# Decode attention with grouped queries: the tokens of one value half are handed out ahead of GpSimd's wait for an output copy, and VectorE counts eight times behind its last sum

## The chip, the cores and the metric

The kernel runs on one core of one Trainium2 chip. The metric is the device time of one execution in microseconds (us), as a median of several executions. One more execution was profiled; all times inside the kernel come from it and count from the start of its span.

## The reference

One token is decoded: 32 query heads of 128 numbers, in 8 groups of 4 heads, each group with its own 65536 keys and values (bf16).

```python
B, Hq, Hkv, Sq, Sk, D = 1, 32, 8, 1, 65536, 128
k = jnp.repeat(k, Hq // Hkv, axis=1)
v = jnp.repeat(v, Hq // Hkv, axis=1)
scores = jnp.einsum("bhqd,bhkd->bhqk", q, k) * D ** -0.5
p = softmax(scores, axis=-1)
return jnp.einsum("bhqk,bhkd->bhqd", p, v)
```

Each key and each value is read once: 268 MB in all.

## The kernel before

**Tiles and their order.** The keys and the values of a group are read in two halves each, here called K(g,0), K(g,1), V(g,0), V(g,1). A half is 256 rows of 128 numbers on each of the 128 partitions, 8.4 MB. They go through a ring of three buffers, `buf`, in the order of the list `tiles` (L153 to L156): K(0,0), K(0,1), K(1,0), K(1,1), V(0,0), and then for each group from 2 on K(g,0), K(g,1), V(g-2,1), V(g-1,0). At the end come V(6,1), V(7,0) and V(7,1). SyncE issues all of these loads, on one queue. Before it issues a load it waits until the half that lies three places earlier has been used up (L163 to L169); for values this is the count `vit`, to which TensorE adds one for every 32 rows that it has consumed (L491).

**The stages of a group.** VectorE turns the keys in place (`turn`, L311), TensorE makes the scores in four PSUM banks (L462), VectorE takes maxima (L371), TensorE and VectorE find each head's maximum (L506, L384), and ScalarE makes the exponentials `E` and their sum (L242). VectorE transposes them into the weights `Ew`, in two halves (L316). TensorE then multiplies weights by values, 4 rows a matmul and 8 matmuls for each pass of the loop `values` (L481 to L494), into `psum_o`; VectorE picks the right blocks of `psum_o` (L324) and sums them (L332); TensorE picks the group's heads (L433), VectorE takes the reciprocal of the sum (L338), and ScalarE scales and writes the group's output (L249), which adds one to `outs`.

**TensorE's order.** TensorE runs these stages as blocks with branches. In turn g it makes the scores of group g, then (from g = 2) uses V(g-2,1), then runs the block `summed` (closing matmul L423, L506, clearing matmul L420, L433), and then uses V(g-1,0). The block `turn` (L516) comes next and takes one count of `wqs`. After V(6,0) there are no more scores: TensorE goes through `turn` and `late` straight to V(6,1), and after V(7,0) likewise to V(7,1). The first 192 rows of V(7,1) run in the loop, its next 40 rows in the block `tail` (L535), and its last 24 rows go one by one (L544).

**Tokens.** Before each pass of `values` TensorE takes one token from `sV` (L482), which stands for 32 rows that have landed. For most halves SyncE adds the eight tokens, in its own stream, when the landing is there (L168). For the last ones, V(6,0), V(6,1) and V(7,0), whose loads are split into 2, 3 and 4 pieces (`BY`), and for the first 4 of the 7 pieces of V(7,1) (`PIECES`, `MOVED`), GpSimd adds them piece by piece as each lands (L216 to L218). All tokens look alike, so those of V(6,0) may not be handed out while TensorE could still take them for V(5,1).

**GpSimd's stream.** GpSimd lays out the queries of group g for the scores once `outs` has reached g (L203 to L213) and adds one to `wqs` each time. Behind the eighth group it waits until `outs` has reached 8, that is until ScalarE has written the output of group 6, adds 2 to `wqs` (L214), and only then begins the list of tokens at L216.

**The end.** VectorE's last block (`last`, L388 to L404) has no loop: it counts on `dl` behind each picking step and waits for it ahead of the sum (L394, L395 and L401, L402). After the last sum TensorE picks group 7's heads, ScalarE scales them (L260) and issues the last store (L264), and counts on `fin` (L265); SyncE counts on `fin` once TensorE is done (L188). GpSimd waits for two counts on `fin` (L557), clears all semaphores (L558) and waits for the stores (L559).

Of the kernel before, what the change touches and what calls it, by code (L numbers as in the profile page):

```python
# [13 lines left out]
G = 8  # L14
# [3 lines left out]
NT = 256  # L18
# [3 lines left out]
BY = {  # L22
    (G - 2, 0): (128, 128), (G - 2, 1): (128, 64, 64), (G - 1, 0): (64, 64, 64, 64),
}
N = 2
STEP = 32
PIECES = (64, 64, 32, 32, 40, 16, 8)
MOVED = 4
# [3 lines left out]
def kernel(  # L32
# [18 lines left out]
    _, Hkv, Sk, _ = k.shape  # L51
# [5 lines left out]
    pe, dve, act, pool, sp = nc.tensor, nc.vector, nc.scalar, nc.gpsimd, nc.sync  # L57
# [38 lines left out]
    def sem(name):  # L96
        sems.append(nc.alloc_semaphore(name))
        return sems[-1]
# [3 lines left out]
    sL = [sem(f"sL{x}") for x in range(sum(map(len, BY.values())))]  # L102
    sP = [sem(f"sP{x}") for x in range(len(PIECES))]
# [5 lines left out]
    vit = sem("vit")  # L109
    scd = sem("scd")  # L110
    vdone = sem("vdone")
    wqs = sem("wqs")
# [7 lines left out]
    outs = sem("outs")  # L120
    rls = sem("rls")
    end = sem("end")
    dl = sem("dl")
# [3 lines left out]
    fin = sem("fin")  # L127
# [75 lines left out]
    for g in range(G):  # L203
# [7 lines left out]
            in1=quad[:, :].unsqueeze(1).unsqueeze(3).broadcast_to([P, 4, 4, H]),  # L211
            op=ALU.mult,
        ).then_inc(wqs, 1)  # L213
    pool.wait_ge(outs, G).then_inc(wqs, 2)  # L214

    for land, n in list(zip(sL, sum(BY.values(), ()))) + list(zip(sP, PIECES))[:MOVED]:  # L216

        pool.wait_ge(land, 32 if land is sP[0] else 16).then_inc(sV, n // STEP)  # L218

    def take(engine, semaphore, n=1):  # L220

        engine.wait_ge(semaphore, n).then_inc(semaphore, -n)  # L222
# [16 lines left out]
    for g in range(G + 1):  # L239
# [8 lines left out]
        at = max(g - 1, 0) * D  # L248
# [3 lines left out]
        if g == 0:  # L252

            for b in range(3):
                n = sum(kind == "k" and at % 3 == b and 0 < h < G - 1 for at, (kind, h, _) in enumerate(tiles))
# [57 lines left out]
    def weights(s):  # L313

        at = slice(1024 * s, 1024 * (s + 1))
        return dve.transpose(out=Ew[:, at], in_=E[:, at])  # L316

    def next_over():

        return dve.tensor_copy(out=rl, in_=rl_next)  # L320

    def picked():

        return dve.tensor_tensor(  # L324
            out=o_m[:, :].rearrange("p (y d) -> p y d", y=4),
            in0=psum_o[:, :].rearrange("p (y d) -> p y d", y=4),
            in1=pick[:, :].unsqueeze(2).broadcast_to([P, 4, D]),
            op=ALU.mult,
        )

    def summed():
        return dve.tensor_reduce(  # L332
            out=o_r[:, 0:D], in_=o_m[:, :].rearrange("p (y d) -> p d y", y=4), axis=AX.X, op=ALU.add
        )

    def over():

        dve.reciprocal(out=rl_next, in_=psum_f[0:H, D:D + 1]).then_inc(rls, 1)  # L338
# [49 lines left out]
    with block("last"):  # L388
        dve.wait_ge(exd, 1)
        dve.wait_ge(vit, NT // STEP * (2 * G - 3))  # L390
        weights(0)
        dve.wait_ge(vdone, 1)
        next_over().then_inc(mxs, 1)
        picked().then_inc(dl, 1)  # L394
        dve.wait_ge(dl, 1)  # L395
        summed().then_inc(mxs, 1)
        weights(1).then_inc(sP[0], 16)
        dve.wait_ge(pes, 2)
        over()
        dve.wait_ge(vdone, 2)  # L400
        picked().then_inc(dl, 1)  # L401
        dve.wait_ge(dl, 2)  # L402
        summed().then_inc(mxs, 1)
        dve.br("done")  # L404


# [49 lines left out]
    with block("scores"):  # L456
# [3 lines left out]
        for y in range(4 * N):  # L460
            m, n = y % 4, y // 4
# [64 lines left out]
    with block("tail"):  # L526
        at = sum(PIECES[:MOVED])
# [26 lines left out]

    pool.wait_ge(fin, 2).then_inc(fin, -2)  # L557
    nc.clear_and_free_semaphores(cleared)  # L558
    pool.wait_ge(sS, 32).then_inc(sS, -32)  # L559

# [29 lines left out]
```

## Time and profile before

| | us |
|---|---|
| median of 3 runs | 632.24 (631.0 to 632.6) |
| the profiled execution | 632.93 |
| its span, first to last instruction | 630.7 |
| TensorE busy (matmul) | 503.5 |
| VectorE busy | 337.9 |
| ScalarE busy | 21.1 |
| GpSimd busy | 5.9 |
| mean granted TensorE clock | 0.935 of full speed |

How to read it: the span is the time from the first to the last instruction in the trace, and the execution's own time is 2.2 us longer. "Busy" is the union of an engine's instructions; register, branch and semaphore instructions aren't in it, so a GpSimd that only hands out tokens counts as idle. PE is TensorE's matmul side and PEld its weight loads, DVE is VectorE, ACT ScalarE, POOL GpSimd, SP SyncE. A q behind an engine's name is its sequencer. L222 is the line of the helper `take`, so "PEq L222" means that TensorE's sequencer stood at such a wait. In a timeline row the square brackets hold the engine's idle time just before the row and what ended it.

### The profile page before, as it was taken

The page shows a single profiled execution, that of the slowest core. Times are in us where ns is not written, and L with a number is a line of the kernel's source. Part 1 is how long each engine was busy: PE and PEld are TensorE (multiplying, and loading weights), DVE is VectorE, ACT ScalarE, POOL GpSimd, SP SyncE. Part 2 cuts the span into 40 slices and gives each one's busy share as a digit, 9 for nine tenths or more (in the row PEclk, how much of TensorE's full clock was granted, in tenths as well). Part 3 has the DMA queues.
Part 4 walks back from the last instruction along what each step waited for, and adds up shares of the span by engine and source line. Part 5 has one row for each costly group of instructions (what it writes and reads, how often), then busy time and mean ns, then how long its engine had stood idle before and what let it go on. Part 6 is the DMA issues. An engine that isn't in the chain of part 4 may idle for free. (4 is left out here: it accounts for less than half of the span.)

```text
span 630.7 us, 8029 instructions
## 1 busy us (share of the span) xinstructions
PE 503.5 (80%) x2189; PEld 204.6 (32%) x2189; DVE 337.9 (54%) x118; ACT 21.1 (3%) x28; POOL 5.9 (1%) x16
## 2 busy tenths in 40 slices
PE   0685398898994979939799398994889987879998
PEld 0232043343331333314333133331333333323333
DVE  3984994789214882158721686217852688210100
ACT  1000100100010000100001000010000100010000
POOL 2000000000000000000000000000000000000000
PEclk9999599798998899988999798997999999898999
DMA  8999999999999999999999999999999999999995
GB/s 368 432 463 403 461 399 466 399 466 399 466 420 445 453 411 461 403 466 399 466 399 466 399 466 399 466 399 466 399 466 399 432 432 466 399 432 431 422 427 217
DMA packets 7000, 268.46 MB, mean 426 GB/s; under 512 B 856, under 2 KB 856, under 8 KB 1112
## 3 DMA queue, kind: packets, MB, share of 16 engines
q1 hardware_dynamic: 6912, 268.44, 98.8%
q10 hardware_dynamic: 88, 0.02, 0.0%
HBM read 268.44 MB, written 0.01 MB: 426 GB/s over the span
## 5 line engine op out<-in xcount | busy, mean ns | idle before, releaser
L311 DVE STREAM_TRANSPOSE buf<-buf 128x8192 f32<-128x8192 f32 x32 | 277.2, 8694 | 84.8 <-DVEq L222 84.8
L462 PE MATMUL sc<-buf,zeros 128*128 x1024 | 244.0, 396 | 0.0
L486 PE MATMUL psum_o<-buf,Ew 128*16 x1008 | 228.1, 385 | 13.6 <-PEq L222 9.7
L462 PEld LDWEIGHTS sc<-buf,zeros 128*128 x1024 | 101.6, 99 | 134.6 <-issue 38.7
L486 PEld LDWEIGHTS psum_o<-buf,Ew 128*16 x1008 | 90.2, 89 | 148.6 <-issue 55.1
L420 PE MATMUL sc<-zeros 128*128 128x512 bf16 x32 | 13.6, 426 | 87.2 <-PEq L222 87.0
L324 DVE TENSOR_TENSOR o_m<-psum_o,pick 128x512 f32<-128x512 f32 x10 | 7.0, 696 | 99.0 <-DVEq L222 72.1
L320 DVE COPY o_r<-o_r 4x1 f32<-4x1 f32 x9 | 1.3, 142 | 76.7 <-DVEq L222 64.1
L420 PEld LDWEIGHTS sc<-zeros 128*128 128x128 bf16 x32 | 3.1, 98 | 96.4 <-issue 95.4
L242 ACT ACTIVATE zeros<-sc,nmb 128x2048 bf16<-128x2048 f32 x8 | 15.7, 1967 | 536.6 <-DVE nmb L384 536.6
L316 DVE STREAM_TRANSPOSE Ew<-zeros 128x1024 bf16<-128x1024 bf16 x18 | 22.3, 1240 | 19.6 <-PE psum_o L486 19.5
L371 DVE TENSOR_REDUCE mx<-sc 128x1 f32<-128x2048 f32 x8 | 18.0, 2252 | 0.0
L506 PE MATMUL misc<-each,same 128*128 128x512 f32 x18 | 10.8, 685 | 8.3 <-PEq L222 8.3
L443 PE MATMUL misc<-qt,rep 32*128 32x128 bf16 x1 | 0.3, 281 | 10.6 <-DVE qt L301 10.6
L420 PE MATMUL psum_o<-zeros 128*128 128x512 bf16 x10 | 4.5, 446 | 5.3 <-PEq L222 5.3
L332 DVE TENSOR_REDUCE o_r<-o_m 128x128 f32<-128x512 f32 x10 | 6.9, 692 | 1.2
L208 POOL TENSOR_TENSOR zeros<-qx,quad 128x64 bf16<-128x64 bf16 x8 | 2.4, 294 | 487.6 <-ACT o_out L249 481.4
L506 PEld LDWEIGHTS misc<-each,same 128*128 128x128 f32 x18 | 2.9, 203 | 8.6 <-issue 8.5
L423 PE MATMUL sc<-zeros 128*128 128x1 bf16 x32 | 5.2, 163 | 0.0
L420 PEld LDWEIGHTS psum_o<-zeros 128*128 128x128 bf16 x10 | 1.0, 98 | 12.8 <-issue 12.6
L287 DVE CAST rep<-ident 32x128 bf16<-32x128 f32 x1 | 2.9, 2877 | 2.7 <-POOL ident L193 2.7
L423 PEld LDWEIGHTS sc<-zeros 128*128 128x128 bf16 x32 | 3.0, 95 | 3.9
(32 smaller groups left out, 37.3 us busy)
## 6 DMA issues: line engine op xcount, KB each, us to landing
buf<-in_k_dram SPq DMA_DIRECT2D x8, 4096.0 KB, 28.4
buf<-in_v_dram SPq DMA_DIRECT2D x8, 2048.0 KB, 34.4
buf<-in_v_dram SPq DMA_DIRECT2D x3, 4096.0 KB, 31.5
buf<-in_v_dram SPq DMA_DIRECT2D x2, 1024.0 KB, 32.7
buf<-in_v_dram SPq DMA_DIRECT2D x1, 1280.0 KB, 36.4
buf<-in_v_dram SPq DMA_DIRECT2D x1, 512.0 KB, 37.2
buf<-in_v_dram SPq DMA_DIRECT2D x1, 256.0 KB, 36.9
buf<-in_k_dram SPq DMA_DIRECT2D x12, 34.6
```

Source lines behind the costliest of these rows:

```text
L242: act.activation(out=E[:, :], in_=sc[:, :], func=ACT.Exp, bias=nmb[:, 0:1], scale=SCALE, accum_out=o_r[:, D:D + 1],).then_inc(exd, 1)
L287: dve.tensor_copy(out=rep[:, :].rearrange("p (a x) -> p a x", a=4), in_=ident[0:32, 0:32].unsqueeze(1).broadcast_to([32, 4, 32]),)
L311: dve.transpose(out=kv, in_=kv).then_inc(kt, 1)
L316: return dve.transpose(out=Ew[:, at], in_=E[:, at])
L324: return dve.tensor_tensor(out=o_m[:, :].rearrange("p (y d) -> p y d", y=4), in0=psum_o[:, :].rearrange("p (y d) -> p y d", y=4), in1=pick ...
L332: return dve.tensor_reduce(out=o_r[:, 0:D], in_=o_m[:, :].rearrange("p (y d) -> p d y", y=4), axis=AX.X, op=ALU.add)
L371: after(dve.tensor_reduce(out=mx[:, :], in_=sc[:, :], axis=AX.X, op=ALU.max))
L420: return pe.matmul(out=bank, lhsT=zer[:, 0:P], rhs=zer[:, :], start=True, stop=False)
L423: return pe.matmul(out=bank[:, 0:1], lhsT=zer[:, 0:P], rhs=zer[:, 0:1], start=False, stop=True)
L462: pe.matmul(out=bank, lhsT=moved(wq[:, m * SLIDE + 4 * n:][:, 0:P], slide), rhs=moved(T[:, n, m // 2, m % 2], keys), start=False, stop=False,)
L486: last = pe.matmul(out=psum_o[0:16, :], lhsT=moved(Ew[:, column(4 * j + 3):][:, 0:16], weight), rhs=moved(buf[:, 4 * j * D:][:, 0:4 * D], ...
L506: pe.matmul(out=misc[:, :], lhsT=same[:, :], rhs=each[:, :].unsqueeze(1).broadcast_to([P, 16, 32]), start=True, stop=True,).then_inc(pes, 1)
```

## The change

GpSimd's wait for `outs` and the 2 counts on `wqs` move from ahead of the list of tokens to behind its second entry, so behind both pieces of V(6,0). In their old place GpSimd now waits until `vit` has reached 8 * (2 * 8 - 4) = 96, that is until TensorE has used up every half as far as V(5,1). VectorE issues eight instructions more behind its last sum, each a bare count: seven on `dl` and one on `fin`. GpSimd's wait at the end asks for three counts on `fin` in place of two.

```diff
@@ GpSimd, behind the loop over the groups
-    pool.wait_ge(outs, G).then_inc(wqs, 2)
-
-    for land, n in list(zip(sL, sum(BY.values(), ()))) + list(zip(sP, PIECES))[:MOVED]:
+
+    pool.wait_ge(vit, NT // STEP * (2 * G - 4))
+    for at, (land, n) in enumerate(list(zip(sL, sum(BY.values(), ()))) + list(zip(sP, PIECES))[:MOVED]):
 
         pool.wait_ge(land, 32 if land is sP[0] else 16).then_inc(sV, n // STEP)
+        if at == 1:
+            pool.wait_ge(outs, G).then_inc(wqs, 2)
@@ VectorE, block "last"
         dve.wait_ge(dl, 2)
         summed().then_inc(mxs, 1)
+
+        for _ in range(7):
+            dve.nop().then_inc(dl, 1)
+        dve.nop().then_inc(fin, 1)
         dve.br("done")
@@ GpSimd, at the end
-    pool.wait_ge(fin, 2).then_inc(fin, -2)
+    pool.wait_ge(fin, 3).then_inc(fin, -3)
```

## The prediction

> **What bounds the kernel now.** I read the page first, for the transfers:
>
> ```profile
> DMA packets 7000, 268.46 MB, mean 426 GB/s; under 512 B 856, under 2 KB 856, under 8 KB 1112
> buf<-in_v_dram SPq DMA_DIRECT2D x1, 1280.0 KB, 36.4
> buf<-in_v_dram SPq DMA_DIRECT2D x1, 512.0 KB, 37.2
> buf<-in_v_dram SPq DMA_DIRECT2D x1, 256.0 KB, 36.9
> ```
>
> The first line says that 268 MB of keys and values fill nearly the whole span (630.7 us) at 426 GB/s. The other three are the last three pieces of V(7,1), the second half of group 7's values (40, 16 and 8 rows). The trace has SyncE issuing them at 585.60, 586.09 and 587.01, so they land at 622.0, 623.3 and 623.9. The span ends 6.8 us after the last landing, so the end isn't the transfers' alone. Hence the second view, TensorE's timeline near the end (start, length, line, what, count, idle before):
>
> ```profile
> 545.95 15.33 PE L486 MATMUL psum_o<-buf,Ew 128*16 x64 [3.05 <-PEq L222]
> 561.21 0.18 PE L423 MATMUL psum_o<-zeros 128*128 128x1 bf16 x1
> 561.25 1.10 PE L506 MATMUL misc<-each,same 128*128 128x512 f32 x2
> 563.22 0.38 PE L420 MATMUL psum_o<-zeros 128*128 128x512 bf16 x1 [0.87 <-PEq L222]
> 563.52 0.38 PE L433 MATMUL psum_f<-o_r,sel 128*4 128x129 f32 x2
> 567.09 30.50 PE L486 MATMUL psum_o<-buf,Ew 128*16 x128 [3.19 <-POOLq L218]
> 597.52 0.18 PE L423 MATMUL psum_o<-zeros 128*128 128x1 bf16 x1
> 600.18 14.19 PE L486 MATMUL psum_o<-buf,Ew 128*16 x64
> 615.39 10.72 PE L486 MATMUL psum_o<-buf,Ew 128*16 x48 [1.01 <-PEq L222]
> 626.27 0.82 PE L535 MATMUL psum_o<-buf,Ew 128*16 128x512 bf16 x10 [0.17 <-issue]
> ```
>
> From 567.09 on TensorE works without a long gap through V(6,0) and V(6,1) (128 matmuls), V(7,0) (64), 192 rows of V(7,1) (48) and the 40 rows of L535. It reaches those 40 rows at 626.27, 4.3 us after they landed. So in the last 60 us TensorE is late and the transfers are ahead. The one avoidable wait in that run is the 3.19 us before 567.09, and the view names what ended it: GpSimd's token at L218.
>
> Third, the stretches around it (busy of each engine, granted TensorE clock, DMA share, GB/s):
>
> ```profile
> 564.04:567.09 3.05, 0.00 (x0) 0.01 (x1) 0.31 (x3) 2.30 (x3) 0.00 (x0) 0.79 1.20 516
> 567.09:572.60 5.51, 5.51 (x14) 1.83 (x15) 0.00 (x0) 0.00 (x0) 0.00 (x0) 0.50 0.88 381
> 572.60:597.50 24.90, 24.90 (x116) 10.27 (x114) 1.25 (x1) 0.00 (x0) 0.00 (x0) 1.00 1.01 431
> ```
>
> After the wait the first 5.5 us run at half clock, 0.43 us a matmul instead of 0.216. So the wait costs more than its own length.
>
> **The change, part by part.**
>
> *The tokens of V(6,0).* Before, GpSimd stands at L214 until ScalarE has scaled group 6's output (that copy ends at 566.63, the wait at 566.67) and hands out tokens at 566.76 and 566.86. Now it waits for the value count 96, which TensorE reaches with the last matmul of V(5,1) at 561.27, then for the landings. In the trace's landing records V(6,0)'s two halves land at 555.3 and 565.0. So the first four tokens are there by about 561.5, before TensorE asks at about 563.8, and the other four at 565.1. When TensorE needs none of this wait, the same step is seen one group earlier:
>
> ```profile
> 489.68 0.17 PE L423 MATMUL psum_o<-zeros 128*128 128x1 bf16 x1
> 491.99 0.38 PE L433 MATMUL psum_f<-o_r,sel 128*4 128x129 f32 x2
> 492.51 14.15 PE L486 MATMUL psum_o<-buf,Ew 128*16 x64
> ```
>
> From L433 to the first value matmul it takes 0.52 us. So V(6,0) starts at 563.52 + 0.52 = 564.04 instead of 567.09: 3.05 us earlier. Half of it takes 7 us, so the second half is wanted at 571, after its landing. ScalarE's exponential (564.33 to 566.30) then lies beside value matmuls; it does so after 492.51 too, and those run at full speed, so I charge nothing.
>
> *The clock.* The trace's clock record changes on a grid of 3.41 us. I laid TensorE's busy time on that grid: after a slot busy 33% or less the clock is halved, after one busy 42% or more it never is. Now TensorE idles 0.87 us before L420 and 0.14 us before 564.04, so the emptiest slot possible is busy 1 - 1.01/3.41 = 70%. No half clock. But the slow start had let TensorE's sequencer run ahead, and this hid the 1.01 us that a change of half costs at 615.39 (it is part of the gap list above; between V(6,0) and V(6,1) before there is none). At full clock that gap returns: V(6,0) to the start of V(6,1) takes 615.39 - 600.18 = 15.21, and from a half's first matmul to the closing one it is 489.68 - 475.43 = 14.25 (475.43 is where V(4,1) starts). So the closing matmul comes at 564.04 + 15.21 + 14.25 = 593.50 instead of 597.52: **4.02 us earlier**. That is 3.05 of wait and 0.97 of clock, net of the new gap.
>
> [...]
>
> *The moved wqs count.* It now stands behind two landings (565.1) and the copy (566.67). TensorE asks for it after V(6,0), at about 578: 11 us of cover. Queued behind it on GpSimd are only tokens for later pieces, the next landing at 574.7. Free.
>
> *What is late next.* V(6,0)'s buffer is free at 578.6 instead of 583.8, so SyncE issues V(7,1)'s seven pieces 5.2 us earlier, into a queue that still holds a quarter of V(6,1) and all of V(7,0). At 561.30 V(7,0) was issued behind about as much, and pieces kept landing every 4.9 us. So I take the landings as unmoved (they could gain only if the queue ran dry, which it doesn't). Against TensorE 4.02 us earlier: V(6,1) is wanted from 579.25, landed 574.7 to 584.5, each a few us in hand; V(7,0)'s last quarter is wanted at 606.7, landed 604.1; V(7,1)'s second piece wanted at 614.9, landed 613.9; the 32-row pieces wanted at 618.4 and 620.1, landed 616.4 and 618.9; the 40 rows wanted at 626.27 - 4.02 = 622.25, landed 622.0. **This margin, 0.26 us, is the thinnest**: a little more and the landings would set the end. The 16 rows would be wanted at 623.11 and land at 623.3: 0.2 us late, beside VectorE's last sum, which runs to 624.64; the 24 small matmuls take 1.3 us to their last start and are issued just as the sum ends. Nothing is added.
>
> *VectorE's eight counts.* Not seen before, so bounds: the nearest rows are ScalarE's three bare counts at L256, each 17 ns, 0.08 us apart, and at the dear end VectorE's 0.69 us reduction L332. I take the first, the same kind of instruction: 8 x 0.08 = 0.6 us. The sum ends at 628.66; ScalarE's own count for the end comes at 629.82, and GpSimd, after clearing, still waits for the store until 630.69, with 0.3 us to spare. So 1.5 us of cover: **nothing**. Were each 0.69, it would be 5.5 - 1.5 = 4 us. [...]
>
> ScalarE's counts at L256 run at 65.9, while the activation that stands before them in the program (L249) starts at 67.8. [...]
>
> **The sum.** The profiled execution took 632.93 us (span 630.7 and 2.2 around it). 632.93 - 4.02 = **628.9 us**; span 626.7. The median shown is 632.24 (631.0 to 632.6). The spread below the profiled one is about what a missing slow start would give (0.97 here, and V(5,1)'s 15.33 against 14.22 is another 1.1). After the change these hardly count, since the 40 rows' landing stops any further gain at 0.26 us. So I keep 628.9 for the median too, 0.5% below 632.24.
>
> **The rivals.**
> 1. *The landings set the end sooner.* The deeper queue, or a slower stream, moves the last pieces by 1 to 3 us. For it: 0.26 us of margin. Against: the steady 4.9 us at equal depth. Time 630 to 632. Chance 0.09, a third of it within 0.3%.
> 2. *The token wasn't what held V(6,0)*, or the half clock returns. If the copy or the exponential were the real condition, nothing changes: 632.2. Against: 492.51 starts before that group's exponential. If only the clock stays halved: 632.93 - 3 = 630. Chance 0.07, most of it no change.
> 3. *Slower: the counts set the end.* Each waits for VectorE's write before it, and GpSimd can't clear until the eighth. It decides past 1.5 + 4.0 = 5.5 us in all, 0.69 each; at the price of VectorE's 1.24 us transposes, 9.9 us, the profiled time is 632.93 + 9.9 - 5.5 = 637.3. Against: the 0.08 us of L256. Chance 0.04.
>
> Forecast 0.80. About 0.3% (1.9 us) is what a measurement can tell from no change. Faster by more: 0.80 + 0.06 + 0.01 = 0.87; within: 0.09; slower: 0.04. The range, 627.6 to 631.0, takes in the forecast with the runs' own spread and most of the first rival; the counts' dear end (4 us) is left out with the third.
>
> **What would show it.** Right: the idle time before L486 in this place is gone and V(6,0) starts 0.5 us after L433; clock 1.00 through it; a new gap of 1.0 us between V(6,0) and V(6,1); closing matmul 4 us earlier; L535 starting within 0.3 us of the 40 rows' landing; last landing at 624. Wrong: landings later than 624, TensorE waiting on L222 among V(7,1)'s pieces, half clock after 564, or GpSimd's L557 released by VectorE.

## The result, and the profile after

The changed kernel takes 628.82 us (median of 4 runs, 628.61 to 629.23), the kernel before 632.42 (4 runs, 631.0 to 633.18): ratio 0.9946, 95% interval 0.9928 to 0.9965. With 26 runs the kernel before stands at 632.1 (631.1 to 633.5). The profiled execution of the changed kernel took 629.23 us, its span is 627.4.

The lines of the changed kernel's code are six further down in the matmul part: L492 is the value matmul that was L486, L429 the closing matmul, L439 the picking one, L541 the 40 rows, L550 the 24 rows, and L224 the helper that waits. TensorE's timeline of the changed kernel, with some short rows left out:

```profile
546.16 15.66 PE L492 MATMUL psum_o<-buf,Ew 128*16 x64 [3.04 <-PEq L224]
561.75 0.18 PE L429 MATMUL psum_o<-zeros 128*128 128x1 bf16 x1
564.07 0.38 PE L439 MATMUL psum_f<-o_r,sel 128*4 128x129 f32 x2
564.56 14.19 PE L492 MATMUL psum_o<-buf,Ew 128*16 x64
579.80 14.22 PE L492 MATMUL psum_o<-buf,Ew 128*16 x64 [1.05 <-PEq L224]
594.04 0.17 PE L429 MATMUL psum_o<-zeros 128*128 128x1 bf16 x1
596.69 14.19 PE L492 MATMUL psum_o<-buf,Ew 128*16 x64
611.90 10.71 PE L492 MATMUL psum_o<-buf,Ew 128*16 x48 [1.01 <-PEq L224]
622.78 0.82 PE L541 MATMUL psum_o<-buf,Ew 128*16 128x512 bf16 x10 [0.17 <-issue]
```

V(6,0) begins 0.49 us behind L439, with no idle time in brackets; before, it was 3.57 us behind. Its 64 matmuls take 14.19 us, and a new gap of 1.05 us stands ahead of V(6,1). From the closing matmul of V(5,1) to that of V(6,1) it is 594.04 - 561.75 = 32.29 us; before it was 597.52 - 561.21 = 36.31. The difference is 4.02 us. The stretch of V(6,0), in the same columns as in the views before, has the whole clock (1.00, the third number from the end):

```profile
564.56:578.80 14.24, 14.19 (x64) 5.60 (x64) 0.34 (x3) 2.30 (x3) 0.00 (x0) 1.00 1.00 430
```

The transfers have not moved. The page of the changed kernel on the last three pieces:

```profile
buf<-in_v_dram SPq DMA_DIRECT2D x1, 1280.0 KB, 41.7
buf<-in_v_dram SPq DMA_DIRECT2D x1, 512.0 KB, 40.6
buf<-in_v_dram SPq DMA_DIRECT2D x1, 256.0 KB, 36.9
```

SyncE issues V(7,1) from 578.78 on instead of 583.81, and the 40 rows are 41.7 us on their way in place of 36.4: they land at 622.3, as before within 0.3 us. Issued earlier, behind transfers that are still under way (V(6,1)'s last piece and the four of V(7,0) land from 584.7 to 604.4), they only wait longer.

### The profile page after: what moved, and what is told of

The parts are those of the page before. It is cut to its first block, busy times and chain, and to the rows that moved or that the text cites. A ratio compares the mean times of both kernels' runs of the same rounds, so it can differ in the third digit from the quotient of the medians.

```text
span 627.4 us, 8037 instructions
## 1 busy us (share of the span) xinstructions
PE 503.3 (80%) x2189; PEld 204.4 (33%) x2189; DVE 337.9 (54%) x118; ACT 21.1 (3%) x28; POOL 5.9 (1%) x16
## 5 line engine op out<-in xcount | busy, mean ns | idle before, releaser
L492 PE MATMUL psum_o<-buf,Ew 128*16 x1008 | 225.1, 381 | 11.6 <-PEq L224 10.7
L492 PEld LDWEIGHTS psum_o<-buf,Ew 128*16 x1008 | 89.3, 89 | 144.4 <-issue 54.0
L429 PE MATMUL sc<-zeros 128*128 128x1 bf16 x32 | 5.2, 164 | 0.0
L429 PEld LDWEIGHTS sc<-zeros 128*128 128x128 bf16 x32 | 3.1, 95 | 3.9
## 6 DMA issues: line engine op xcount, KB each, us to landing
buf<-in_v_dram SPq DMA_DIRECT2D x1, 1280.0 KB, 41.7
```

The costliest lines, as they stand in the source:

```text
L429: return pe.matmul(out=bank[:, 0:1], lhsT=zer[:, 0:P], rhs=zer[:, 0:1], start=False, stop=True)
L492: last = pe.matmul(out=psum_o[0:16, :], lhsT=moved(Ew[:, column(4 * j + 3):][:, 0:16], weight), rhs=moved(buf[:, 4 * j * D:][:, 0:4 * D], ...
```

## The experiments

**The tokens alone.** VectorE's counts are taken out of the changed kernel.

```diff
-        for _ in range(7):
-            dve.nop().then_inc(dl, 1)
-        dve.nop().then_inc(fin, 1)
-    pool.wait_ge(fin, 3).then_inc(fin, -3)
+    pool.wait_ge(fin, 2).then_inc(fin, -2)
```

> The changed kernel without VectorE's eight counts (two counts on fin at the end, as before). Theory: the tokens of V(6,0) do all of it and the counts are hidden, so the time is the changed kernel's, 628.8 us, ratio to before 0.994 to 0.995. Rival: the counts give a part of the gain (an earlier last sum), then this is slower than the changed kernel by up to 0.1 us per guarded step, 0.2 us in all; if they carry the gain, it comes out at 632.4.

Measured: 628.81 us (5 runs, 628.45 to 629.04), ratio to before 0.9952 (0.9938 to 0.9966). That is the changed kernel's time to 0.01 us. The tokens carry the gain.

**The counts alone.** The same lines are added to the kernel before.

> The kernel before with VectorE's eight counts alone. Theory: they lie beside the last sum, the last output copy and the last store, so nothing changes: 632.4 us, ratio 1.000 within 0.003. Rival: they delay GpSimd's last wait, then up to 4 us more (0.69 each less 1.5 of cover); or they give a gain of their own, then below 631.

Measured: 631.8 us (11 runs, 631.31 to 633.01), ratio 0.9998 (0.9989 to 1.0008). The counts neither cost nor gain anything. Its trace holds a second finding. The wait is there, and so is half clock, but for one slot of the clock record (3.41 us) instead of the two of the profiled execution before. First its timeline, with some short rows left out:

```profile
563.56 0.38 PE L437 MATMUL psum_f<-o_r,sel 128*4 128x129 f32 x2
567.13 29.45 PE L490 MATMUL psum_o<-buf,Ew 128*16 x128 [3.19 <-POOLq L218]
596.60 0.17 PE L427 MATMUL psum_o<-zeros 128*128 128x1 bf16 x1
```

Then two stretches of its V(6,0); the granted clock is the third number from the end:

```profile
567.13:570.00 2.87, 2.87 (x7) 0.99 (x8) 0.00 (x0) 0.00 (x0) 0.00 (x0) 0.50 0.85 365
570.00:573.00 3.00, 3.00 (x15) 1.27 (x14) 0.00 (x0) 0.00 (x0) 0.00 (x0) 0.97 1.22 524
```

V(6,0) and V(6,1) take 596.60 - 567.13 = 29.47 us to the closing matmul. At whole clock with the gap of 1 us between them it is 594.04 - 564.56 = 29.48 in the changed kernel. So in this execution the slow start (3.07 us at half clock, to the end of that slot) costs nothing: the sequencer's lead that it gives hides the gap. The sequencer takes V(6,1)'s first token at 582.09 here, before the last matmul of V(6,0) starts (582.23); in the changed kernel it takes it at 579.52, 1.15 us after that matmul's start (578.37). The slow start of the kernel before, 5.52 us at half clock, costs 30.43 - 29.48 = 0.95 us.

**Forty counts.** With 32 counts more, the counts should outlast the time that covers them.

```diff
-        for _ in range(7):
+        for _ in range(39):
             dve.nop().then_inc(dl, 1)
```

> The changed kernel with 40 counts in place of 8 (39 on dl, one on fin). In the changed kernel's trace the counts lie 0.093 us apart and the last comes at 625.56, with ScalarE's own count at 626.33. Theory: 32 more at 0.093 are 3.0 us, the last count comes at about 628.5, GpSimd's clearing takes 0.5 behind it, so the span ends at about 629.1 in place of 627.4: 630.5 us, 1.7 over the changed kernel. Rival 1: the pause of 0.5 us that lies between the fourth and the fifth count comes back every four counts, then 4 us more: 634.5. Rival 2: the end doesn't wait for VectorE at all: 628.8.

Measured: 630.45 us (10 runs, 629.9 to 630.73), 1.63 us over the changed kernel; expected were 1.7. In its trace the last count comes at 627.46 and GpSimd passes its wait at 627.52, 2.2 us behind ScalarE's own count (625.35). In the changed kernel the last count comes at 625.56, 0.77 us ahead of ScalarE's. The counts on `dl` (L408) and GpSimd's wait (L563) in this trace:

```profile
L408 DVEq EVENT_SEMAPHORE  x39: 21/21/21, 623.4 to 627.4; - x39
L563 POOLq EVENT_SEMAPHORE  x1: 17/17/17, 627.5 to 627.5; - x1
```

So VectorE does hold the end once it is the last, each count costs 0.093 us, and eight are too few. The pause of 0.50 us that stands between the fourth and the fifth count of the changed kernel (last section) doesn't recur: 37 steps of 0.093 us and one of 0.50 make 3.9 of the 4.0 us between the first and the last count on `dl`.

**The wait kept, the clock kept whole.** The kernel before gets products of zeros while it waits ahead of V(6,0).

```diff
-        pe.br_ne(g, 1, on_true="values", on_false="turn")
+        pe.br_eq(g, G, on_true="warm", on_false="cool")
+    with block("warm"):
+        for _ in range(14):
+            pe.matmul(out=psum_o[:, :], lhsT=zer[:, 0:P], rhs=zer[:, :], start=False, stop=False)
+        pe.br("values")
+    with block("cool"):
+        pe.br_ne(g, 1, on_true="values", on_false="turn")
```

> The kernel before, but TensorE adds 14 products of zeros to psum_o (3.0 us) while it waits for GpSimd's token ahead of V(6,0); the token comes as late as before. It tells the clock's part from the wait's. Theory: no half clock behind the wait, the gap of 1.0 us between V(6,0) and V(6,1) is there, the closing matmul is 0.8 to 1.0 us earlier than before, 631.5 us in an execution that would have had the whole slow start, 632 as a median; the 3.0 us of the wait stay. Rival 1: the half clock is most of the cost, then 2.5 us less than before, 630. Rival 2: the clock doesn't matter: 632.4.

Measured: 631.16 us (11 runs, 630.69 to 632.41), ratio 0.999 (0.9981 to 1.0). The medians differ by 0.9 us, the interval just reaches no change, so only the trace settles the size. Its timeline:

```profile
562.18 0.38 PE L433 MATMUL psum_f<-o_r,sel 128*4 128x129 f32 x2
562.50 3.19 PE L518 MATMUL psum_o<-zeros 128*128 128x512 bf16 x14
565.75 14.20 PE L486 MATMUL psum_o<-buf,Ew 128*16 x64
581.00 14.21 PE L486 MATMUL psum_o<-buf,Ew 128*16 x64 [1.05 <-PEq L222]
595.23 0.17 PE L423 MATMUL psum_o<-zeros 128*128 128x1 bf16 x1
```

V(6,0) begins 565.75 - 562.18 = 3.57 us behind L433, exactly as late as before, but at full clock (1.00):

```profile
565.75:580.00 14.25, 14.20 (x64) 5.60 (x64) 0.00 (x0) 0.00 (x0) 0.00 (x0) 1.00 0.99 422
```

To the closing matmul it is 29.48 us in place of 30.43: the clock's part is 0.95 us. The wait's part stays in, and the kernel stays 2.3 us above the changed one (its added branch costs about 0.27 us of that: 0.79 in place of 0.52 from L433 to V(7,0)). As a median 632 was expected; the measured one is 0.8 below that. The profiled execution, 630.77, was low in part because V(5,1) too ran at full clock in it (14.21 us, 15.33 before), which the added products don't touch; the other runs have no trace.

**Half of the value products left out, changed kernel and kernel before.**

```diff
-        for j in range(STEP // 4):
+        for j in range(STEP // 8):
```

> The changed kernel with 4 in place of 8 value matmuls in each pass of the loop; it leaves out half of the values' products there and reads everything still. TensorE has some 25 us less to do from V(6,0) on. Theory: the landings now set the end, so TensorE stands waiting for the 40 rows of V(7,1) and takes them as they land (0.5 us earlier than in the changed kernel's trace): 628.3 us. Rival: TensorE still sets the end of the changed kernel, then well below 626.

> The kernel before with the same half of the value matmuls left out. Theory: the same floor as with the changed kernel, 628.3 us, since the landings are the same and the late token no longer matters when TensorE has time in hand: that is what the wait costs on TensorE's path and nowhere else. Rival: the late token costs by way of V(7,1)'s later issue, then 3 to 4 us over the other half kernel, 632.

Measured: 628.52 us (4 runs, 628.35 to 629.0) for the changed kernel, 628.98 (6 runs, 628.21 to 629.86) for the kernel before. Expected were 628.3 for both. Three of the six runs of the kernel before stop there (628.2 to 628.4); the other three took 629.6 to 629.9, and no trace shows why. The rival's 632 is far from all of them. The 40 rows in each timeline, the changed kernel's half first, then that of before:

```profile
622.18 0.82 PE L541 MATMUL psum_o<-buf,Ew 128*16 128x512 bf16 x10 [1.78 <-DMA buf<-in_v_dram]
```

```profile
621.61 0.82 PE L535 MATMUL psum_o<-buf,Ew 128*16 128x512 bf16 x10 [1.23 <-DMA buf<-in_v_dram]
```

In both, TensorE stands waiting and the landing ends the wait. So the floor of this order of loads is about 628.5 us. The changed kernel's median lies 0.3 above it, which is less than the spread of its runs.

That the late token cost anything by way of V(7,1)'s later issue these two runs don't test: with half of the products gone V(6,0)'s buffer comes free early in both, and the kernel before then issues V(7,1) from 570.44 on, earlier than the changed kernel. The page of its run shows how long the 40 rows were on their way:

```profile
buf<-in_v_dram SPq DMA_DIRECT2D x1, 1280.0 KB, 43.5
```

It is the traces together that speak against this rival. V(7,1)'s issue begins at 570.44 here, at 578.78 in the changed kernel and at 583.81 in the kernel before, and the 40 rows land at 621.6, 622.3 and 622.0.

**One more wait kept busy.** The changed kernel gets 12 products of zeros in a block between `second` and `values`, ahead of V(g-2,1) in each group.

```diff
-        pe.br_lt(g, 2, on_true="summed", on_false="values")
+        pe.br_lt(g, 2, on_true="summed", on_false="warm")
+    with block("warm"):
+        for _ in range(12):
+            pe.matmul(out=psum_o[:, :], lhsT=zer[:, 0:P], rhs=zer[:, :], start=False, stop=False)
+        pe.br("values")
```

> The changed kernel, but TensorE adds 12 products of zeros to psum_o (2.6 us) ahead of V(g-2,1) in each group, so that the clock stays whole through the 3.0 us wait for V(5,1)'s landing. Theory: V(5,1) takes 14.2 in place of 15.7 us, TensorE reaches the 40 rows 1.4 us earlier, but they have landed only 0.5 us before it gets there now: 0.3 to 0.5 us less, 628.4. Rival: TensorE still sets the end alone: 1.4 less, 627.4.

Measured: 628.56 us (6 runs, 628.26 to 628.83), 0.26 under the changed kernel; the runs of the two overlap, so this is not clear of noise. Its trace shows why it can't be more:

```profile
546.05 14.19 PE L496 MATMUL psum_o<-buf,Ew 128*16 x64 [0.28 <-PEq L224]
614.36 7.17 PE L496 MATMUL psum_o<-buf,Ew 128*16 x32 [0.25 <-PEq L224]
622.12 0.82 PE L545 MATMUL psum_o<-buf,Ew 128*16 128x512 bf16 x10 [0.59 <-DMA buf<-in_v_dram]
```

V(5,1) takes 14.19 us in place of 15.66, as meant, but TensorE then waits for the second piece of V(7,1) and again for the 40 rows. What it gains ahead it gives back to the landings.

## Why the prediction came out as it did

It gave 628.9 us; 628.8 was measured, well inside its range. That the two agree to 0.1 us is partly luck: the sum was made for an execution with two slow slots, and the profiled execution after the change took 629.23, which is 3.70 under 632.93 and not 4.02. Step by step:

- *The wait of 3.05 us.* Right. V(6,0) began 0.49 us behind the picking matmul (0.52 forecast), and the tokens alone give the whole gain. The output copy that the token stood behind is group 5's, and not group 6's as the text before says. It ends at 566.63 in the kernel before, when TensorE had not used any of V(6,0) yet.
- *The clock's 0.97 us, net of the new gap.* Right for the execution that it was worked out from: 0.95 in the kernel kept busy, and the new gap is 1.05 (1.01 forecast). For the median it is too much: the kernel with the counts alone shows an execution where a slow start costs nothing. The medians moved by 3.3 to 3.6 us, not 4.02. The forecast for the median held since the time after hardly depends on it, as the prediction argued from the landing of the 40 rows: the first four runs of the kernel before spread over 2.2 us, the four of the changed kernel over 0.6.
- *The clock's grid.* Right. The clock's steps fall on a grid of 3.41 us in the changed kernel's trace as in that of the kernel before. The grid's offset from the span's start is 2.59 us in the profiled execution before and 0.48 in the changed kernel's. In the kernel with the counts alone the half clock ends at 570.20, which on such a grid is an offset of about 0.2, and there one slot behind the wait was slow in place of two.
- *The landings unmoved, 0.26 us of margin.* Right in kind; TensorE was to be within 0.3 us of the landing. In the changed kernel's trace TensorE reached the 40 rows 0.5 us after their landing, because V(5,1) ran 15.66 us there (15.33 before) and set TensorE back; in the kernel with the tokens alone it reached them at 622.12, 0.3 after the landing at 621.8. The kernels with half of the products show that the landings are the floor.
- *The moved wqs count and the earlier issue of V(7,1): nothing.* Right. GpSimd gives the count at 567.2, TensorE asks behind V(6,0) at 578.8. The landing after it comes at 575.0, in the kernel before at 574.7.
- *The counts: nothing.* Right in effect, and their size was off. 0.08 us each and 0.6 in all were taken; it was 0.093 each from the fifth on and 1.07 from the first to the last, since there is a pause after the fourth (below). The cover was large enough, and forty counts use it up. A gain from a sum that starts early, the rival in the run of the tokens alone, isn't there: the sum starts 0.03 us behind its product with the counts (624.48) and without them (623.82). Where VectorE's neighbours overlap in the trace of the kernel before, it is by 0.07 to 0.09 us, set-up aside.
- *The slower rival* was half right in its mechanism: GpSimd does wait for the last count, as forty of them show, but the counts don't each wait for VectorE's write before them, since four come at 624.49 to 624.79, while the sum runs to 625.17. Its price was too high by a factor of 13 (1.24 us against 0.093).

## What to carry to other kernels

A wait in one engine's stream also holds everything written behind it (here GpSimd's first token came at 566.76, 0.1 us behind its wait at 566.67, for a piece that had landed at 555.3): look for tokens that stand behind a wait they don't need, and when they are moved ahead, put the weakest wait that keeps them apart from the older ones in its place. Price an idle stretch of TensorE with what the trace's clock shows behind it (here 5.5 us at half clock behind a wait of 3.2), then check what the slow start was hiding; here a gap of 1.05 us came back when it went. And before taking a gain upstream at its full size, compare each later arrival with the new time at which it is wanted: here 4.0 us of gain left the median about 0.3 us above the floor that the landings set, and the next 1.5 us bought nothing that could be measured.

## What the runs showed of the hardware that was not expected

In the changed kernel's trace four of VectorE's bare counts come while the sum ahead of them still runs, and the fifth doesn't. The sum runs from 624.48 to 625.17; counts come at 624.49, 624.59, 624.69 and 624.79, the fifth only at 625.28, 0.11 us after the sum's end, and then they go on every 0.093 us. The run with forty counts has room for one such pause in its 4.0 us (above). The first count came 0.01 us after the sum's start and none before the sum's own wait was over, although VectorE had stood idle for 26.8 us ahead of the picking step. So here the first four tell nothing of the sum's end; what makes the fifth wait the trace doesn't show, and no run was made for it.

TensorE's clock was halved also after slots that were far from idle. In the trace of the kernel before, ten slots of the grid at whole clock were followed by half clock, busy 0 to 33% (the fullest from 145.95 to 149.36); those that were followed by whole clock were busy 42% or more (the emptiest from 299.55 to 302.96). In the changed kernel's trace it was ten slots too, busy 0 to 40% (38.03 to 41.44), and the others 43% or more (222.35 to 225.76). Slots at half clock that were followed by whole clock were busy 81% or more before and 86% or more in the changed kernel, those followed by half clock up to 65% and 69%. This is counted from TensorE's matmul records, whose ends the profile models.
